# Layer 1: the low weights of two feature tiles side by side in the array's rows

## The chip, the cores and the metric

The kernel runs on one core of a Trainium2 chip. The metric is device time in microseconds of one execution, as the median of several. A profiled execution gives a trace of every instruction, and the line numbers (L508) are those of the kernel's source before the change. The engines are TensorE (PE for matmuls, PEld for weight loads), VectorE (DVE), ScalarE (ACT), GpSimd (POOL) and SyncE (SP, which here only issues transfers).

## The reference

An input of 2048 tokens by 576 features is normalised; a state-space convolution over the tokens (A) and a two-layer perceptron with another normalisation ahead of it (B) both work on the normalised input, and their results are multiplied.

```python
def _A_ref(u, log_A_real, A_imag, C_real, C_imag, log_dt, D_skip):
    ...
    P = jnp.exp((A * dt[:, None])[:, :, None] * pos[None, None, :])
    K = 2.0 * jnp.einsum("dn,dnl->dl", C, P).real
    ...
    y = jnp.fft.irfft(Uf * Kf[None, :, :], L2)[:, :, :L]
    ...
    return y + u * D_skip[None, None, :]

def _B_ref(x, w1, b1, w2, b2):
    y = _layernorm(x, axis=-1)
    h = _gelu(jnp.einsum("bsd,df->bsf", y, w1) + b1)
    return jnp.einsum("bsf,fd->bsd", h, w2) + b2

x = A_u
xn = _layernorm(x, axis=-1)
s = _A_ref(xn, ...)
g = _silu(_B_ref(xn, B_w1, B_b1, B_w2, B_b2))
return x + s * g
```

w1 is 576 x 4608 and w2 4608 x 576.

## The kernel before

**The perceptron.** To keep float32 accuracy in the fast matmul type, each operand is split into a high part (rounded) and a low part (the rest), and a product is taken as high x high, high x low and low x high. The tokens come in two halves of 1024, each half in two blocks of 512 (`tb` 0 and 1). The 4608 hidden features come in `NG` = 12 groups of `G` = 3 feature tiles of 128. One *slot* is one group with one token block, so there are 48 slots: for each half, for each group, `tb` 0 and then 1.

A slot has 11 positions. Positions 0 to 2 are layer 1 of feature tiles 0 to 2 (`layer1`, L508): 14 matmuls of 128 x 128 weights with 512 tokens each. The 576 input features are four full blocks of 128 and a rest of 64. The full blocks take 3 x 4 = 12 matmuls. For the rest the block `XR` holds the high part of the 64 rows in partitions 0 to 63 and their low part in 64 to 127, and there are two sets of weights: `w1r` has the high weights twice, so one matmul gives high x high and high x low; `w1s` has the low weights in partitions 0 to 63 and zeros below, so a second matmul gives low x high. Positions 3 to 10 are layer 2 (`layer2`, L565): 72 matmuls of 288 output columns for four token tiles j = 0 to 3, summed into `acc` by DVE (L573). The first group of a half adds the bias tile `bias2` instead of `acc`.

Layer 1 and layer 2 share two double banks of PSUM, `mxa` and `mxb`, by turns. Tile 0 and tile 2 of a slot use the two halves of one of them, tile 1 the other. Tile 1's is the one that token tile j = 3 of the slot before has used; it is free once the sum L573 of j = 3 is done.

**The convolution** is done in six chunks of 96 features with small matmuls in array tiles of 32 or 64 rows and columns, or 128 x 32: tables (`kgen`, L885, line `kl`), forward transforms (L958, line `c1`), second stage (L996, `c1`), inverse (L1049, `c3`) and last stage (L1076, `c3`). They are put as *visits* between the positions of a slot.

**The order** of all engines is fixed by a planner, `Order`, as the program is built. It keeps a clock for each engine (`od.t`), marks for finished steps (`od.marks`) and due times (`by`). TensorE's own sequence of positions is written out in the loop over slots at the end; `od.unit` puts down a block of matmuls with its planned length (`L1` for a feature tile, `LEN` for a position), `od.advance` puts down what other engines can do up to a time, and `pe_turns` makes the visits that are ready. All kinds of visits are allowed after positions 0, 1, 2, 4, 6, 8 and 10. `later(slot, pos, f)` runs f after a position.

Weights come from HBM through a ring `raw`, issued by SP (`load_raw`), and are split by ACT and DVE (`split_raw`, L485 and L488).

Of the kernel before, what the change touches and what calls it, by code (L numbers as in the profile page):

```python
# [9 lines left out]
F32 = mybir.dt.float32  # L10
F32R = mybir.dt.float32r
# [6 lines left out]
L, D, N, F = 2048, 576, 128, 4608  # L18
P = 128
# [19 lines left out]
TB = 512  # L39
# [173 lines left out]
def mixer_kernel(ctx, tc, u, log_a_real, a_imag, c_real, c_imag, log_dt, d_skip, w1, b1, w2, b2,  # L213
                 f1, f2, g2, g1, tvals, ident, out, parts=("mlp", "s4d")):
    nc = tc.nc
    sb = ctx.enter_context(tc.tile_pool(name="sb", bufs=1))
# [5 lines left out]
    def bank2(name):  # L222
        return ps.tile([P, 2, TB], F32, name=name, bufs=2 if name == "cv" else 1)

    def dram(ap_of, offset, ap):
        return bass.AP(tensor=ap_of.tensor, offset=ap_of.offset + offset, ap=ap)
# [22 lines left out]

    idt = ys_tile().rearrange("p i a b c -> p (i a b c)")[:, :P]  # L250
    idp = sb.tile([P, P], F32, name="idp")
    bias2 = sb.tile([P, D], F32, name="bias2")
    f1t = sb.tile([P, 2, 32], F32, name="f1t")
    g1t = sb.tile([P, 32], F32, name="g1t")
    tvs = sb.tile([P, NV + 7], F32, name="tv")
# [2 lines left out]
    halfpi, epst = small[:, 0:2], small[:, 2:4]  # L258
    dsk = sb.tile([P, D // 4], F32, name="dsk")
    w1s = sb.tile([P, G * P], F32R, name="w1s")  # L260

    def load_tv():
        for k in range(2):
# [51 lines left out]
    nc.vector.memset(halfpi, TWO_PI / 4)  # L315
    nc.vector.memset(epst[:, 0:1], EPS)
    nc.vector.memset(epst[:, 1:2], EPS * EPS)
    nc.vector.memset(w1s[64:].bitcast(F32), 0.0)
    nc.vector.memset(dsk, 0.0)


# [1 line left out]
    acc = sb.tile([P, 8, D], F32, name="acc")  # L323
# [77 lines left out]
    XR = sb.tile([P, 2, TB], F32R, name="XR")  # L401
# [27 lines left out]
    W = {}  # L429
# [33 lines left out]
    def split_raw(low_on=nc.vector):  # L463
        k = state["split"]
        state["split"] += 1
        half, g, which, i = PARTS[k]
        r = RAW.pop(k)
        if which == 1:
            if i == 0 and k:
                w1_tiles()  # L470
            h, lo, r1, r2 = W[1]
            if i < KB:
                h, lo = h[:, i], lo[:, i]
                m = P
            else:
                h, lo = r1, r2[:64]
                m = 64
        else:
            if i == 0:
                W[2] = (sb.tile([P, G, D], F32R, name="w2h"), sb.tile([P, G, D], F32R, name="w2l"))  # L480
            h, lo = W[2]
            h, lo, m = h[:, i], lo[:, i], P

        def low():
            low_on.tensor_sub(lo, r[:m], h[:m].bitcast(F32))  # L485
            for _ in range(NEXT[which - 1][i]):
                load_raw()
        nc.scalar.activation(h, r, AF.Copy)  # L488
        return low

    HID, LAST, Q1, Q2 = {}, {}, {}, {}
    turn = [0]

    def mx(i):
        return "mxa" if (turn[0] + i) % 2 == 0 else "mxb"

    def layer1(g, tb, i):
        h, lo, r1, r2 = W[1]
        c = slice(i * P, (i + 1) * P)
        if i < 2:  # L500
            Q1[i] = bank2(mx(i))
        q = Q1[i % 2][:, i // 2]
        ops = []
        for a, b in ((h, XH), (h, XL), (lo, XH)):
            ops += [(a[:, kb, c], b[:, kb, tb]) for kb in range(KB)]
        ops += [(r1[:, c], XR[:, tb]), (r2[:, c], XR[:, tb])]
        for j, (a, b) in enumerate(ops):
            nc.tensor.matmul(q, a, b, start=j == 0, stop=j == len(ops) - 1)  # L508
        return hidden(g, tb, i, q)

    def first_layer1(i):


        h, lo, r1, r2 = W[1]
        if i != 1:
            Q1[i] = bank2("mxb" if i else "mxa")
        q = Q1[2][:, 0] if i == 2 else Q1[0][:, i]
        pairs = [(h, XH, 0), (h, XH, 1), (h, XL, 0), (h, XH, 2), (h, XL, 1), (h, XH, 3), (h, XL, 2), (h, XL, 3)]

        if i != 1:  # L520
            for j, (a, b, kb) in enumerate(pairs):
                for k in ((0, 1), (2,))[i // 2]:
                    nc.tensor.matmul(Q1[k // 2 * 2][:, k % 2], a[:, kb, k * P:(k + 1) * P], b[:, kb, 0],  # L523
                                     start=j == 0, stop=False)
        c = slice(i * P, (i + 1) * P)
        for kb in range(KB):
            nc.tensor.matmul(q, lo[:, kb, c], XH[:, kb, 0], start=False, stop=False)
        for r in (r1, r2):
            nc.tensor.matmul(q, r[:, c], XR[:, 0], start=False, stop=r is r2)

        return [hidden(0, 0, k, Q1[k // 2 * 2][:, k % 2]) for k in ((), (0, 1), (2,))[i]]
# [18 lines left out]
    def layer2(g, tb, j, terms, last, alone=False):  # L550

        h, lo = W[2]
        hh, hl = HID[tb]
        c = slice(j * P, (j + 1) * P)
        if alone and terms[0][1]:
            Q2[j] = bank2("cv")
        elif j not in Q2:
            Q2[j] = bank2(mx(j + 1))  # L560
        q = Q2[j]
        for i, dh in terms:
            d = slice(dh * 288, dh * 288 + 288)
            for k, (a, b) in enumerate(((hh, h), (hh, lo), (hl, h))):
                nc.tensor.matmul(q[:, dh, :288], a[:, i, c], b[:, i, d], start=i == 0 and k == 0,  # L565
                                 stop=i == G - 1 and k == 2)
        if last:
            Q2.pop(j)

        def add(dh, n):  # L570
            o = acc[:, tb * 4 + j].rearrange("p (h d) -> p h d", h=2)[:, dh:dh + n]
            b = bias2.rearrange("p (h d) -> p h d", h=2)[:, dh:dh + n]
            nc.vector.tensor_add(o, q[:, dh:dh + n, :288], b if g == 0 else o)  # L573
        return add

    def tanh_half(z):
# [529 lines left out]
    NPOS = G + 8  # L1106
    NSLOT = 4 * NG
    od = Order(tc, nc)
    od.pinned = True
    el, wl2, wl, nl2, pl, pl2, pl3, pl4, pl5, nl, ml, ml2, xl, wx, c3, c2, c1, kl, tl, sl, vl, gl, fl, f2l = [od.line() for _ in range(24)]  # L1110
# [8 lines left out]
        load_raw()  # L1119
    for b in range(4, 8):  # L1120
        x_load(b)
    nc.sync.dma_start(bias2, dram(b2, 0, [[0, P], [1, D]]))

    zero = XL[:, KB - 1, 0]
    nc.gpsimd.memset(zero.bitcast(F32), 0.0)
# [58 lines left out]
    L1 = 14 * 0.2275  # L1184
    LEN = [L1] * G + [3 * n * 0.133 for n in (4, 2, 2, 4, 3, 3, 3, 3)]
# [86 lines left out]
    def x_free(tb):  # L1272
        od.marks["free", tb] = od.t["PE"] + od.LAT
        del od.marks["x", tb]
# [31 lines left out]
    def wmark(n, which):  # L1306

        per = KB + 1 + G
        a = n * per + (0 if which == 1 else KB + 1)
        return [("w", k) for k in range(a, a + (KB + 1 if which == 1 else G))]  # L1310
# [20 lines left out]
    part = {}  # L1331
    for k in range(4):
        gl["steps"].append(step("POOL", 5.0, lambda k=k: part.update({k: load_g2(k)}), mark=("g2", k),
                                need=[("g2c", k - 1)] if k else []))
# [37 lines left out]
    def pe_turns(limit=1, any_time=False, all_lines=True):  # L1372
        for x in (nl, pl, ml) + ((c3, c1, kl) if all_lines else ()):
            n = 0
            while n < (2 if x in (c1, nl) else limit):
                h = od.head(x)
                if h is None or h[0]["eng"] != "PE" or h[1] > od.t["PE"] + (0.3 if x is nl else -0.4):
                    break
                if x is c1:
                    now = od.t["PE"]  # L1380
                    gap = (END - now) / max(pace["left"], 1)
                    if n == 0 and pace["started"] and now < pace["last"] + 0.4 * gap and not any_time:
                        break
                    pace["started"], pace["last"] = True, now
                    pace["left"] -= 1
                if x is kl and pace["started"] and kl["steps"][0]["mark"][1] < NB - 1 and od.t["PE"] < h[1] + ALONE:
                    break
                behind = ride(h[0]) if x is c1 or x is c3 and h[0]["mark"][0] == "i1" else None
                od.run(x)
                if behind:  # L1390
                    behind()
                od.pin()
                od.advance(od.t["PE"])
                n += 1

    LATER = {}

    def later(slot, pos, f):
        LATER.setdefault((slot, pos), []).append(f)
    mid = 2 * NG  # L1400

    later(mid - 3, 0, block_lines)
    later(mid - 2, G - 1, lambda: x_free(0))
    later(mid - 1, G - 1, lambda: x_free(1))
    later(NSLOT - 10, 4, end_line)
# [41 lines left out]
    for slot in range(NSLOT):  # L1447
        turn[0] = slot + 1
        g, tb = slot // 2 % NG, slot % 2
        n = slot // 2  # L1450
        final = slot >= NSLOT - 2
        for pos in range(NPOS):
            if pos < G:
                need = wmark(n, 1) + [("x", tb)]
                if pos == 0:
# [4 lines left out]
                    if slot in (1, 2 * NG + 1):  # L1460
                        od.marks["x", tb] -= 2.3
                cell = []
                od.unit(lambda: cell.extend([layer1(g, tb, pos)] if slot else first_layer1(pos)),
                        L1 if slot else L1 * (22, 6, 14)[pos] / 14, need)
                look_ahead(pos)
                for k, (a, b, c) in enumerate(cell, pos + 1 - len(cell)):
                    by = hidden_by(pos, k)
# [6 lines left out]
            else:  # L1474
                j, terms, last, hid = l2_terms(pos - G)
                need = [wmark(n, 2)[i] for i in hid] + [("h", slot, i) for i in hid]
# [29 lines left out]
            for f in LATER.get((slot, pos), ()):  # L1506
                f()
            od.advance(od.t["PE"])
            pe_turns(all_lines=pos in (0, 1, 2, G + 1, G + 3, G + 5, NPOS - 1))
    od.force(lambda: not od.urgent and not any(x["steps"] for x in od.lines))  # L1510


# [52 lines left out]
```

## Time and profile before

| | |
|---|---|
| median of 3 runs | 1084.04 us (1083.93 to 1084.64) |
| profiled execution: its own time | 1084.01 us |
| profiled execution: its span, first to last instruction | 1082.2 us |
| mean granted TensorE clock | 0.998 |
| DVE busy | 945.4 us (87%) |
| ACT busy | 652.2 us (60%) |
| transfers | 125.55 MB, mean 116 GB/s |

The span is what the rows of the profile are measured in. Busy time counts each instruction from its start to its end, with overlapping ones joined; a matmul's end is modelled, so for TensorE the distance between starts tells more than the duration. In a group's row stand line, engine, operation, output and inputs, rows by columns of the array tile, shape, count, then busy time and mean duration in ns. In a timeline's row stand start and length in us; xN joins N like instructions. A wait's row has total, times and longest in us.

### The profile page before, as it was taken

Reading aid. Unit: us, or ns where it says so; the run is one execution under the profiler, and the core shown is the slowest. Engines: PE = TensorE matmul, PEld = TensorE weight load, DVE = VectorE, ACT = ScalarE, POOL = GpSimd, SP = SyncE. Lnnn points to the kernel's source line nnn. Section 1 sums busy time; section 2 is a strip of 40 time slices with the busy share of each in tenths; the row PEclk is TensorE's granted clock in tenths of the full one; section 3 lists DMA queues with packets and bytes.
Section 4 is the critical chain, followed back from the end, with each engine's and each line's share of the span. In section 5 each row is a group of like instructions: output and inputs, shape, how many; then the busy total and the mean of one; then the engine's idle time right before and its main releaser. Section 6 shows DMA issues by size and latency. Waiting matters only on the chain.

```text
span 1082.2 us, 27218 instructions
## 1 busy us (share of the span) xinstructions
PE 1073.0 (99%) x11507; PEld 935.6 (86%) x11507; DVE 945.4 (87%) x1520; ACT 652.2 (60%) x974; POOL 197.1 (18%) x282
## 2 busy tenths in 40 slices
PE   9999999999999999999999999999999999999997
PEld 7889989888888888898888888889888888888896
DVE  7799688988999998999999998998999897677266
ACT  6666678767576576557657767566665653233233
POOL 5592631111000100002100020000100013110420
PEclk9999999999999999999999999999999999999999
DMA  8654567424133321634525131241412347441623
GB/s 252 226 163 166 196 219 203 123 68 144 36 113 67 91 88 40 138 73 112 153 77 128 35 104 54 75 117 25 117 52 76 121 78 227 126 122 53 217 76 88
DMA packets 129371, 125.55 MB, mean 116 GB/s; under 512 B 78821, under 2 KB 100913, under 8 KB 128225
## 3 DMA queue, kind: packets, MB, share of 16 engines
q1 hardware_dynamic: 113584, 76.44, 25.4%
q0 software_dynamic: 15104, 46.49, 13.8%
q8 instruction: 90, 1.47, 0.5%
q10 hardware_dynamic: 560, 0.89, 0.3%
q14 instruction: 33, 0.26, 0.1%
HBM read 95.52 MB, written 34.01 MB: 120 GB/s over the span
## 4 chain that ended last, share of the span: by engine, by line
PE 97%; DVE 2%; ACT 0%; issue 0%; DMA 0%; ACTq 0%
PE mxa L508 21%; PE mxb L565 21%; PE mxb L508 21%; PE mxa L565 21%; PE cv L885 3%; PE cv L996 3%; PE cv L1049 2%; PE cv L958 2%; PE cv L1076 1%; PE mxa L523 0%; DVE st L371 0%; PE cv L413 0%; DVE row L386 0%; DMA acc<-in_A_u_dram 0%; DVE A L644 0%
## 5 line engine op out<-in xcount | busy, mean ns | idle before, releaser
L565 PE MATMUL mxb<-w2h,hh 128*128 128x288 f32 x576 | 171.7, 298 | 0.0
L565 PE MATMUL mxa<-w2h,hh 128*128 128x288 f32 x573 | 170.5, 297 | 0.0
L565 PE MATMUL mxb<-w2h,hl 128*128 128x288 f32 x576 | 170.2, 296 | 0.0
L565 PE MATMUL mxb<-w2l,hh 128*128 128x288 f32 x576 | 169.5, 294 | 0.0
L565 PE MATMUL mxa<-w2h,hl 128*128 128x288 f32 x573 | 169.1, 295 | 0.0
L565 PE MATMUL mxa<-w2l,hh 128*128 128x288 f32 x573 | 168.6, 294 | 0.0
L547 DVE TENSOR_TENSOR hl<-h,hh 128x512 fp32r<-128x512 f32 x144 | 98.8, 688 | 77.6 <-ACT hh L544 76.6
L541 ACT ACTIVATE h<-mxa,b1t 128x512 f32<-128x512 f32 x73 | 50.1, 688 | 125.5 <-PE mxa L508 123.6
L785 POOL DMA_DIRECT2D par<-par_s x36 | 27.4, 761 | 520.4 <-DVE mg L828 511.5
L565 PEld LDWEIGHTS mxa<-w2h,hh 128*128 128x128 f32 x573 | 107.6, 188 | 8.4 <-issue 4.1
L565 PEld LDWEIGHTS mxb<-w2h,hh 128*128 128x128 f32 x576 | 108.2, 188 | 6.8 <-issue 2.4
L565 PEld LDWEIGHTS mxb<-w2l,hh 128*128 128x128 f32 x576 | 108.2, 188 | 0.6
L565 PEld LDWEIGHTS mxb<-w2h,hl 128*128 128x128 f32 x576 | 108.1, 188 | 0.2
L565 PEld LDWEIGHTS mxa<-w2l,hh 128*128 128x128 f32 x573 | 107.6, 188 | 0.6
L565 PEld LDWEIGHTS mxa<-w2h,hl 128*128 128x128 f32 x573 | 107.5, 188 | 0.0
L541 ACT ACTIVATE h<-mxb,b1t 128x512 f32<-128x512 f32 x71 | 48.8, 687 | 79.9 <-PE mxb L508 79.0
L544 ACT ACTIVATE hh<-h 128x512 fp32r<-128x512 f32 x144 | 90.9, 632 | 4.2
L573 DVE TENSOR_TENSOR acc<-mxa,acc 128x576 f32<-128x576 f32 x88 | 65.4, 743 | 18.0 <-PE mxa L565 17.9
L508 PE MATMUL mxa<-XH,w1h 128*128 128x512 f32 x284 | 79.0, 400 | 0.0
L488 ACT ACTIVATE w2h<-raw 128x576 fp32r<-128x576 f32 x72 | 44.2, 674 | 56.6 <-PE mxa L565 56.4
L508 PE MATMUL mxb<-XH,w1h 128*128 128x512 f32 x280 | 77.8, 399 | 0.0
L508 PE MATMUL mxa<-XL,w1h 128*128 128x512 f32 x284 | 76.2, 390 | 0.0
(240 smaller groups left out, 2454.3 us busy)
## 6 DMA issues: line engine op xcount, KB each, us to landing
raw<-in_B_w_dram SPq DMA_DIRECT2D x72, 288.0 KB, 3.1
raw<-in_B_w_dram SPq DMA_DIRECT2D x96, 192.0 KB, 3.2
par_s<-A POOLq DMA_DIRECT2D x8, 1080.0 KB, 4.7
par<-par_s POOLq DMA_DIRECT2D x36, 240.0 KB, 3.3
f2t<-f2q SPq DMA_DIRECT2D x24, 256.0 KB, 3.4
raw<-in_B_w_dram SPq DMA_DIRECT2D x48, 96.0 KB, 3.9
xc<-xn_s SPq DMA_DIRECT2D x48, 96.0 KB, 3.7
u_s<-in_A_u_dram POOLq DMA_DIRECT2D x16, 288.0 KB, 4.4
```

Source lines behind the costliest of these rows:

```text
L488: nc.scalar.activation(h, r, AF.Copy)
L508: nc.tensor.matmul(q, a, b, start=j == 0, stop=j == len(ops) - 1)
L541: nc.scalar.activation(t, q, AF.Gelu_apprx_tanh, bias=b1t[:, g * G + i:g * G + i + 1], scale=1.0)
L544: LAST[0] = nc.scalar.activation(hh[:, i], t, AF.Copy)
L547: nc.vector.tensor_sub(hl[:, i], t, hh[:, i].bitcast(F32))
L565: nc.tensor.matmul(q[:, dh, :288], a[:, i, c], b[:, i, d], start=i == 0 and k == 0, stop=i == G - 1 and k == 2)
L573: nc.vector.tensor_add(o, q[:, dh:dh + n, :288], b if g == 0 else o)
L785: nc.gpsimd.dma_start(PAR[b].rearrange("p (g i) k -> p g (i k)", g=4), dram(par_s, (b // 6 * CH + b % 6 * 4) * NPAR, [[D * NPAR, P], [24 * ...
L885: nc.tensor.matmul(q[32 * g:32 * g + 32, i // 2, i % 2 * 64:i % 2 * 64 + 64], U[:, ri, 4 * g + i, :], v[:, ri, 4 * g + i, :], start=ri == ...
L958: nc.tensor.matmul(Q1ST[i, x][g // 2][64 * f:64 * f + 64, g % 2].rearrange(order), f1t[r].rearrange("p s k -> p (s k)"), rhs(r, f), start= ...
L996: nc.tensor.matmul(Q[i][32 * q:32 * q + 32, f, 2 * ri:2 * ri + 2], m[r, 4 * i + q, 32 * ri:32 * ri + 32], A2[r, 4 * p + 2 * i + q // 2, :, ...
L1049: nc.tensor.matmul(QI[q // 2][64 * f:64 * f + 64, q % 2, i], MAT["g2t", p + i // 2][r, i % 2, ri], YS[p + i // 2][0][r, i % 2, ri, f], sta ...
```

## The change

For some pairs of feature tiles the two low matmuls (`w1s` with `XR`) are taken out of their tiles and done together, as two matmuls of 64 rows that use the upper and the lower half of the array's rows: tile a from partitions 0 to 63, tile b from 64 to 127. So `w1s` holds the low weights in both halves of its partitions (the zeros go), and a second copy of the 64 high rows of `XR` lies in partitions 64 to 127 of a new tile, brought there by a transfer from SBUF to SBUF for each slot (`rows_again`). In a tile that is not paired, the matmul of `w1s` has all 128 rows as before, and adds the product low x low.

A pair is placed only where a visit of `kl`, `c1` or `c3` is the last thing that `pe_turns` has made: after position 0 (tiles 1 and 2 of the slot) or after position 10 (tiles 0 and 1 of the slot that follows; this asks for the sum of token tile 3). It comes first in its tiles' sums (`start=True`), and the tiles have 13 matmuls left. The copy is issued after position 1 of the slot before, for slots 3 to 22 and 27 to 47. Its tile takes the place of `bias2` in memory, so the bias is loaded once more in slot 23, ahead of the second half's first group.

```diff
-    bias2 = sb.tile([P, D], F32, name="bias2")
...
+    def bias_load():
+        PART["b2"] = sb.tile([P, D], F32, name="part")
+        nc.sync.dma_start(PART["b2"], dram(b2, 0, [[0, P], [1, D]]))
...
-    nc.vector.memset(w1s[64:].bitcast(F32), 0.0)
...
-                h, lo = r1, r2[:64]
-                m = 64
+                h, lo = r1, r2
+                m = P
...
+    def tile1(slot, i):
+        if (slot, i) not in OPEN:
+            if i < 2:
+                Q1[i] = bank2("mxa" if (slot + 1 + i) % 2 == 0 else "mxb")
+            OPEN[slot, i] = [Q1[i % 2][:, i // 2], False]
+        return OPEN[slot, i]
+
+    def side_by_side(slot, a, b):
+
+        tb = slot % 2
+        for i in sorted((a, b)):
+            tile1(slot, i)[1] = True
+        for i, r, x in ((a, slice(0, 64), XR[:64, tb]), (b, slice(64, P), PART["x2"][64:])):
+            nc.tensor.matmul(OPEN[slot, i][0], W[1][3][r, i * P:(i + 1) * P], x, start=True, stop=False)
+
+    def rows_again(slot):
+
+        if "x2" not in PART:
+            PART["x2"] = sb.tile([P, D], F32R, name="part")[:, 32:32 + TB]
+        nc.sync.dma_start(PART["x2"][64:].bitcast(F32), XR[:64, slot % 2].bitcast(F32))
+        od.marks["x2", slot] = od.t["PE"] + X2LOAD
+        od.pin()
...
-        ops += [(r1[:, c], XR[:, tb]), (r2[:, c], XR[:, tb])]
+        ops += [(r1[:, c], XR[:, tb])] + ([] if begun else [(r2[:, c], XR[:, tb])])
         for j, (a, b) in enumerate(ops):
-            nc.tensor.matmul(q, a, b, start=j == 0, stop=j == len(ops) - 1)
+            nc.tensor.matmul(q, a, b, start=j == 0 and not begun, stop=j == len(ops) - 1)
...
+                SEEN[0] = x is c3 or x is c1 or x is kl
                 n += 1
+
+    SEEN = [False]
+    X2LOAD, PAIR1 = 4.5, 0.33
+
+    def pair_up(slot, a, b, need):
+        now = od.t["PE"]
+        need = need + [("x2", slot), ("x", slot % 2)] + wmark(slot // 2, 1)
+        if not SEEN[0] or (slot, a) in OPEN or not all(od.marks.get(m, 1e9) <= now for m in need):
+            return
+        od.unit(lambda: side_by_side(slot, a, b), PAIR1, need)
+        for i in (a, b):
+            LEN[i] = L1 * 13 / 14
+        od.advance(od.t["PE"])
...
+    for s in [*range(2, mid - 2), *range(mid + 2, NSLOT - 1)]:
+        later(s, 1, lambda s=s: rows_again(s + 1))
+    later(mid - 1, 1, bias_again)
...
             od.advance(od.t["PE"])
+            SEEN[0] = False
             pe_turns(all_lines=pos in (0, 1, 2, G + 1, G + 3, G + 5, NPOS - 1))
+            if pos == 0:
+                pair_up(slot, 1, 2, [])
+            elif pos == NPOS - 1:
+                pair_up(slot + 1, 0, 1, [("acc", slot, 3, 0)])
```

More of the change, by code (lines that the diff above doesn't have):

```diff
@@ L260, in mixer_kernel @@
     w1s = sb.tile([P, G * P], F32R, name="w1s")
+    PART = {}
+    def bias_load():
+        PART["b2"] = sb.tile([P, D], F32, name="part")
+        nc.sync.dma_start(PART["b2"], dram(b2, 0, [[0, P], [1, D]]))
     def load_tv():
@@ L495, in mx, with layer1 @@
         return "mxa" if (turn[0] + i) % 2 == 0 else "mxb"
-    def layer1(g, tb, i):
+    OPEN = {}
+    def tile1(slot, i):
[16 more added lines that the diff above has]
+        od.pin()
+    def layer1(slot, g, tb, i):
         h, lo, r1, r2 = W[1]
         c = slice(i * P, (i + 1) * P)
-        if i < 2:
-            Q1[i] = bank2(mx(i))
-        q = Q1[i % 2][:, i // 2]
+        q, begun = tile1(slot, i)
         ops = []
@@ L571, in add @@
             o = acc[:, tb * 4 + j].rearrange("p (h d) -> p h d", h=2)[:, dh:dh + n]
-            b = bias2.rearrange("p (h d) -> p h d", h=2)[:, dh:dh + n]
-            nc.vector.tensor_add(o, q[:, dh:dh + n, :288], b if g == 0 else o)
+            b = PART["b2"].rearrange("p (h d) -> p h d", h=2)[:, dh:dh + n] if g == 0 else o
+            nc.vector.tensor_add(o, q[:, dh:dh + n, :288], b)
         return add
@@ L1121, in mixer_kernel @@
         x_load(b)
-    nc.sync.dma_start(bias2, dram(b2, 0, [[0, P], [1, D]]))
+    bias_load()
     zero = XL[:, KB - 1, 0]
@@ L1400, in mixer_kernel, with bias_again @@
     mid = 2 * NG
+    def bias_again():
+        PART.pop("x2")
+        bias_load()
+        od.pin()
     later(mid - 3, 0, block_lines)
+    for s in [*range(2, mid - 2), *range(mid + 2, NSLOT - 1)]:
+        later(s, 1, lambda s=s: rows_again(s + 1))
+    later(mid - 1, 1, bias_again)
     later(mid - 2, G - 1, lambda: x_free(0))
@@ L1462, in mixer_kernel @@
                 cell = []
-                od.unit(lambda: cell.extend([layer1(g, tb, pos)] if slot else first_layer1(pos)),
-                        L1 if slot else L1 * (22, 6, 14)[pos] / 14, need)
+                od.unit(lambda: cell.extend([layer1(slot, g, tb, pos)] if slot else first_layer1(pos)),
+                        LEN[pos] if slot else L1 * (22, 6, 14)[pos] / 14, need)
+                LEN[pos] = L1
                 look_ahead(pos)
```

## The prediction

> **What bounds the kernel now.** I read the page's busy table and its chain of waits first, because they say which engine a saved instruction has to be on.
>
> ```profile
> PE 1073.0 (99%) x11507; PEld 935.6 (86%) x11507; DVE 945.4 (87%) x1520; ACT 652.2 (60%) x974; POOL 197.1 (18%) x282
> ...
> PE 97%; DVE 2%; ACT 0%; issue 0%; DMA 0%; ACTq 0%
> ```
>
> TensorE is busy 99% of the 1082.2 us span and carries 97% of the chain that ends last. So a matmul taken away shortens the run by what it occupies, and one put in lengthens it. The longest entry in the view of PE's waits agrees, 1.3 us before the warm-up at the start:
>
> ```profile
> PE mxa L1131 <- POOL XL L1125: 1.3, 1, 1.3
> ```
>
> DVE at 87% is not the bound, but it can become one for single waits.
>
> Next, the groups by form, for the instructions that the change is about, the products of `w1s`:
>
> ```profile
> L508 PE MATMUL mxa<-XR,w1s 128*128 128x512 f32 x71 | 27.6, 389 | 0.0
> ...
> L508 PE MATMUL mxb<-XR,w1s 128*128 128x512 f32 x70 | 27.2, 388 | 0.0
> ```
>
> 141 of them, one for each feature tile of slots 1 to 47. The 389 ns is latency: matmuls overlap. What one occupies is the distance from start to start, and that comes from the timeline of TensorE, here one tile before a convolution visit (L958), the visit, and the tile after it:
>
> ```profile
> 220.26 0.39 PE L508 MATMUL mxa<-XR,w1r 128*128 128x512 f32 x1
> 220.49 0.39 PE L508 MATMUL mxa<-XR,w1s 128*128 128x512 f32 x1
> 220.81 0.90 PE L958 MATMUL cv<-xc,f1t 32*64 32x384 f32 x16
> 221.64 1.20 PE L508 MATMUL mxb<-XH,w1h 128*128 128x512 f32 x4
> 222.67 1.07 PE L508 MATMUL mxb<-XL,w1h 128*128 128x512 f32 x4
> 223.58 1.07 PE L508 MATMUL mxb<-XH,w1l 128*128 128x512 f32 x4
> 224.49 0.39 PE L508 MATMUL mxb<-XR,w1r 128*128 128x512 f32 x1
> 224.72 0.39 PE L508 MATMUL mxb<-XR,w1s 128*128 128x512 f32 x1
> 224.94 0.29 PE L565 MATMUL mxa<-w2h,hh 128*128 128x288 f32 x1
> ```
>
> Three things stand in these rows. In the stream four matmuls take 223.58 - 222.67 = 0.91 us, so one takes 0.2275. From the last full matmul to the visit's first there are 220.81 - 220.49 = 0.32 us, 0.09 more than 0.2275: going over to another shape of tile costs 0.09. And after the visit the first four need 222.67 - 221.64 = 1.03, 0.12 more than 0.91: the first weights of a new shape can't be loaded under a running matmul.
>
> **What a pair saves and costs.** It saves two matmuls of the stream, 2 x 0.2275 = 0.455 us (the two tiles then have 13 each). It adds two matmuls of 64 rows by 128 columns. The trace has few of that shape, L693, and they show what the change of rows alone costs:
>
> ```profile
> 37.48 0.40 PE L508 MATMUL mxa<-XR,w1s 128*128 128x512 f32 x1
> 37.72 0.60 PE L692 MATMUL cv<-ys,kt 128*128 128x128 f32 x4
> 38.25 0.27 PE L693 MATMUL cv<-ys,kt 64*128 64x64 f32 x1
> 38.45 0.73 PE L508 MATMUL mxb<-XH,w1h 128*128 128x512 f32 x2
> ```
>
> From L508 to L692 the shape stays and the distance is the ordinary one (0.24). The four L692 last 0.60 with 0.27 for the last, so they start (0.60 - 0.27) / 3 = 0.11 apart and the last at 38.05; L693, with the same 128 columns and half the rows, comes 0.20 later, 0.09 too late. From L693 back to L508 it is 0.20 again for half as long a stream (0.055): a switch and weights loaded in the open. And the second L508 then starts at 38.45 + 0.73 - 0.39 = 38.79, 0.34 after the first, 0.11 more than 0.2275. So 128 to 64 rows is a switch, in both directions.
>
> A visit is followed by one switch now (visit to full array, 0.09, first weights 0.11). With a pair it is followed by two: visit to 64 rows, then 64 rows to the full array. The first takes the place of the present one. The pair's own bill is therefore: its first weights in the open 0.11, one stream of 512 elements for both 0.21 to 0.2275, the second's later start 0.01, and one more switch 0.09; the full tile's first weights lay open before as well. Sum 0.42 to 0.44, I take 0.43. Gain per pair 0.455 - 0.43 = 0.025 us: nearly all of the saving goes into the second switch and the open weights. The planner's own price, PAIR1 = 0.33, holds the open weights and one stream, and no second switch.
>
> That the halves run at once I take from the visit above: 16 matmuls of 384 elements pass in 221.64 - 220.81 = 0.83 us with the switch; one after another, at L692's 0.11 for 128, they would need 16 x 0.33 = 5.3. These are of another number type and half as fast per element, so a pair at full rate is not shown.
>
> **How many pairs.** They are made only where a convolution visit (kl, c1 or c3) is the last thing after tile 0 or at the end of a slot, in slots that have the copy: 3 to 22 and 27 to 47. I counted along the timeline, 42 products of L508 and 72 of L565 to a slot. After tile 0 there are 14 such visits, the first and the last being
>
> ```profile
> 195.04 1.10 PE L885 MATMUL cv<-v,U 128*32 128x64 f32 x64
> ...
> 1000.36 1.61 PE L1076 MATMUL cv<-A,g1t 64*32 64x384 f32 x32
> ```
>
> At slot ends there are 9, three of them ahead of slots already counted (a slot gets one pair), 20 slots in all. The first and the last of the 9 begin with
>
> ```profile
> 395.95 1.10 PE L885 MATMUL cv<-v,U 128*32 128x64 f32 x64
> ...
> 974.40 1.60 PE L996 MATMUL cv<-A,f2t 64*32 64x192 f32 x64
> ```
>
> At a slot's end the pair also asks that the sum of the last token tile (L573) be done, since it frees tile 1's bank. Two visits, of TensorE and then of DVE:
>
> ```profile
> 906.90 0.90 PE L958 MATMUL cv<-xc,f1t 32*64 32x384 f32 x16
> 907.73 0.50 PE L508 MATMUL mxb<-XH,w1h 128*128 128x512 f32 x1
> ...
> 488.37 1.10 PE L885 MATMUL cv<-v,U 128*32 128x64 f32 x64
> 489.40 0.50 PE L508 MATMUL mxb<-XH,w1h 128*128 128x512 f32 x1
> ```
>
> ```profile
> 907.01 0.76 DVE L573 TENSOR_TENSOR acc<-mxa,acc 128x576 f32<-128x576 f32 x1 [2.46 <-PE mxa L565]
> ...
> 489.10 0.74 DVE L573 TENSOR_TENSOR acc<-mxa,acc 128x576 f32<-128x576 f32 x1
> ```
>
> In the first the sum ends at 907.77, 0.04 after the visit; in the second at 489.84, 0.44 after it, and the planner would refuse that pair. The longer visits cover the sum. So I take 19 pairs: 19 x 0.025 = 0.5 us gained. The new wait at slot ends, with the whole of the tile's matmuls queued behind it on TensorE, I put at 0.1 us in two or three places where the planner's clock is a little off: 0.2 us back. Its bounds are 0 and 0.44 at six of the nine slot ends, the planner refusing the rest, 2.6 us.
>
> **What is hidden.** 41 copies of 64 rows by 2 KB (128 KB each) go through SP's queue. The nearest issue, and the longest entry of that queue's own waits:
>
> ```profile
> g2t<-g2p SPq DMA_DIRECT2D x24, 128.0 KB, 3.1
> ...
> SPq L448 <- DVE w1l L485: 395.4, 25, 33.0
> ```
>
> A landing takes about 3 us, and the copy is issued after tile 1 of the slot before: tile 2, 14 x 0.2275 = 3.2 us, and all of layer 2 lie between it and the pair. It waits for the pair that last read the tile, which stands earlier in TensorE's order; behind it on SP are the weight loads of `raw`, and these sit waiting for DVE (395 us in all, the second row), so they lose nothing. If that cover were gone, a copy that is late by its landing would cost 3 us at one pair. The bias comes back by one more load, in slot 23 for slot 24, a slot ahead. The fill of `w1s` that goes away and the low half, now 128 rows instead of 64 with as many elements in each, cost DVE and POOL what they did or less:
>
> ```profile
> L485 DVE TENSOR_TENSOR w1s<-raw,w1r x23: 541/544/549, 49.9 to 1032.2; 64x384 fp32r<-64x384 f32 x23
> ...
> L318 DVE MEMSET w1s<- x1: 378/378/378, 1.1 to 1.1; 64x384 f32 x1
> ```
>
> 0.378 us at 1.1 us, when TensorE only warms up: nothing. A pair at a slot's end needs the new weights' low part 3 us earlier than now. The planner asks for it too, and it is split a whole layer 2 before. What is left is the order of other work, which the planner writes anew from its altered clock. Each stop of TensorE costs 0.09 + 0.09 + 0.11 = 0.29 us, so three stops more or less are 0.9 us, either way.
>
> The sum goes against the profiled execution's own time, 1084.01 us (span 1082.2); the median of the runs shown, 1084.04, is the same to 0.03. 1084.0 - 0.5 + 0.2 = 1083.7 us.
>
> **The rivals.** First, the second switch or the open weights are hidden. A pair is then 0.32 to 0.34, gains 0.12, 19 x 0.12 = 2.3 us: 1081.7. For it speaks that weights of other tiles in the same shape are loaded together in the visits; against it the L692, L693, L508 rows, where each change of rows shows its 0.09.
>
> Second, a pair costs no more than one matmul, 0.2275 + 0.01, and gains 0.22: 19 x 0.22 = 4.2, 1079.8 us. The Trainium skill, "TensorE: Matmul & The Clock Gate", Part 3, has this rule: tiles in different row groups take the span of one matmul and about 4 ns for each further one. By that rule the second rival's time would come out; the rows of L693 speak against it at this place, as the pair stands between two changes of shape.
>
> Third, slower: the halves run one after the other, because full-rate streams of 512 into two banks are not taken side by side. A pair is then 0.43 + 0.2275 = 0.66, loses 0.2, 19 x 0.2 = 3.9: 1087.9 us. A pair makes the kernel slower from 0.455 up, and by over 0.2% from 0.455 + 2.17 / 19 = 0.57. Against it speak the 0.83 us of the sixteen; for it, that no row has such a pair.
>
> Fourth, the pairs are rarely made, as the planner's clock leaves out most places: 1084.0, no change. It lies inside the forecast.
>
> **How the numbers follow.** 0.2% is 2.17 us, about what a measurement of this kernel can tell from no change. Forecast with the fourth rival 0.60, of which 0.52 lie within 2.17 us and 0.08 above it, from slot-end waits near their bound with a worse order of stops. First rival 0.20, of which 0.17 faster by over 0.2% and 0.03 within, its 2.3 us being so near to 2.17. Second 0.05, faster; third 0.15, slower. Faster 0.17 + 0.05 = 0.22, same 0.52 + 0.03 = 0.55, slower 0.08 + 0.15 = 0.23. The range 1081.2 to 1087.0 takes in the first rival, and above it the waits' bound of 2.6 us with three more stops (1084.0 - 0.5 + 2.6 + 0.9). It leaves out the second rival and the third at its full price: 2 in 10.
>
> **What would show it.** In the timeline after: 64-row matmuls of `w1s` with `part` behind visits, some 19 times two. The distance from the pair's first start to the next full matmul's start should be 0.42 to 0.44, with both halves starting 0.01 apart. 0.33 means the first rival, 0.24 the second, 0.65 the third. Matmuls of the full `w1s` should fall from 141 by twice the number of pairs. I am wrong if the pair's distance is outside 0.38 to 0.50, if PE's waits show DVE L573 or the copy for more than 1 us in all, or if the number of stops moves by more than five.

## The result and the profile after

The changed kernel takes 1087.21 us (median of 9 runs) against 1084.04 us before: the ratio is 1.003, 95% interval 1.0021 to 1.0039. It is slower, and lies 0.2 us above the range; the forecast was 1083.7. (Ratios leave disturbed runs out, so they can differ a little from the quotient of two medians.) The profiled execution took 1087.15 us, its span is 1085.4 us, 3.2 longer than before.

The page's busy table and the engines of its chain:

```profile
PE 1073.5 (99%) x11507; PEld 931.1 (86%) x11507; DVE 945.0 (87%) x1519; ACT 654.1 (60%) x976; POOL 197.1 (18%) x282
...
PE 94%; DVE 2%; ACT 2%; issue 1%; DMA 0%; ACTq 0%; DVEq 0%
```

TensorE still sets the time, but its share of the chain has gone from 97% to 94%, and ScalarE now has 2% where it had none. The groups by form show how many pairs there are (L535 is the old L508, L516 the pair):

```profile
L535 PE MATMUL mxa<-XR,w1s 128*128 128x512 f32 x48 | 18.7, 389 | 0.0
...
L535 PE MATMUL mxb<-XR,w1s 128*128 128x512 f32 x47 | 18.3, 388 | 0.0
...
L516 PE MATMUL mxa<-XR,w1s 64*128 64x512 f32 x12 | 6.0, 498 | 0.0
L516 PE MATMUL mxb<-part,w1s 64*128 64x512 f32 x12 | 5.9, 493 | 2.2 <-ACT h L568 2.2
L516 PE MATMUL mxb<-XR,w1s 64*128 64x512 f32 x11 | 5.5, 499 | 0.0
L516 PE MATMUL mxa<-part,w1s 64*128 64x512 f32 x11 | 5.4, 495 | 0.0
```

23 pairs, and 141 - 46 = 95 whole low matmuls. One of the pair's groups has idle time before it, 2.2 us, and what ended it is the GELU (ACT, L568). The waits of TensorE say the same:

```profile
PE mxb L516 <- ACT h L568: 2.2, 3, 1.0
PE cv L417 <- DVE U L385: 1.4, 1, 1.4
PE mxa L1158 <- POOL XL L1152: 1.3, 1, 1.3
```

The first row did not exist before. The second is of the start-up, before the first matmuls of layer 1, where the kernel before waited 0.6 us for DVE. Two pairs in the timeline of TensorE, one of the ordinary kind and one of those three, and ScalarE beside the second:

```profile
195.23 1.10 PE L912 MATMUL cv<-v,U 128*32 128x64 f32 x64
196.26 0.50 PE L516 MATMUL mxb<-XR,w1s 64*128 64x512 f32 x1
196.26 0.50 PE L516 MATMUL mxa<-part,w1s 64*128 64x512 f32 x1
196.69 0.73 PE L535 MATMUL mxb<-XH,w1h 128*128 128x512 f32 x2
...
217.78 0.90 PE L985 MATMUL cv<-xc,f1t 32*64 32x384 f32 x16
218.61 0.50 PE L516 MATMUL mxa<-XR,w1s 64*128 64x512 f32 x1
220.12 0.49 PE L516 MATMUL mxb<-part,w1s 64*128 64x512 f32 x1 [1.01 <-ACT h L568]
220.54 0.73 PE L535 MATMUL mxa<-XH,w1h 128*128 128x512 f32 x2
```

```profile
216.93 1.14 ACT L847 ACTIVATE w<-w,tv 128x1024 f32<-128x1024 f32 x1
218.08 1.28 ACT L568 ACT_TABLE_LOAD   x1
219.38 0.69 ACT L568 ACTIVATE h<-mxb,b1t 128x512 f32<-128x512 f32 x1
```

The ordinary pair: both halves start together, and the next full matmul 196.69 - 196.26 = 0.43 us later. The other one: the second half starts at 220.12, 1.51 us after the first, and 0.05 after the end of the GELU at 219.38 + 0.69 = 220.07. That GELU reads the sum of tile 0, which lies in one bank of `mxb`; the waiting matmul writes tile 2's sum into the other bank of the same double bank. The GELU is late since ScalarE had a 1024-element piece of the tables and a table load of 1.28 us ahead of it.

The view of waits counts only 1.01 us there, because the first half's modelled end covers 0.5 of it. From start to start the three late pairs lose 1.50, 0.87 and 1.28 us, 3.65 in all:

```profile
309.64 0.50 PE L516 MATMUL mxa<-XR,w1s 64*128 64x512 f32 x1
310.50 0.49 PE L516 MATMUL mxb<-part,w1s 64*128 64x512 f32 x1 [0.37 <-ACT h L568]
...
496.79 0.50 PE L516 MATMUL mxa<-XR,w1s 64*128 64x512 f32 x1
498.07 0.49 PE L516 MATMUL mxb<-part,w1s 64*128 64x512 f32 x1 [0.78 <-ACT h L568]
```

Two more pairs after tile 0 were held for a moment, by 0.09 and 0.02 us from start to start, too little for the view of waits. The longer of them, TensorE and then ScalarE:

```profile
891.74 0.50 PE L516 MATMUL mxb<-XR,w1s 64*128 64x512 f32 x1
891.83 0.49 PE L516 MATMUL mxa<-part,w1s 64*128 64x512 f32 x1
```

```profile
891.09 0.69 ACT L568 ACTIVATE h<-mxa,b1t 128x512 f32<-128x512 f32 x1
```

Here too the second half starts 0.05 us after the GELU's end, 891.83 against 891.78, as it does at all five places. The five pairs at slot ends wait for nothing: their halves start 0.003 us apart, and the waits for DVE's sum that were expected there are not seen.

The sum is then 1084.04 - 23 x 0.025 + 3.65 + 0.11 (the two short waits) = 1087.2 us. That it meets the measured time to 0.1 us is partly luck: in the profiled executions the first tile of slot 1 starts at 34.64 us, 0.20 later than before, and the sum does not have that.

### The profile page after: what moved, and what is told of

Its sections match the earlier page's. It is cut to its first block, busy times and chain, and to the rows that moved or that the text cites. A ratio compares the mean times of both kernels' runs of the same rounds, so it can differ in the third digit from the quotient of the medians.

```text
span 1085.4 us, 27304 instructions
## 1 busy us (share of the span) xinstructions
PE 1073.5 (99%) x11507; PEld 931.1 (86%) x11507; DVE 945.0 (87%) x1519; ACT 654.1 (60%) x976; POOL 197.1 (18%) x282
## 4 chain that ended last, share of the span: by engine, by line
PE 94%; DVE 2%; ACT 2%; issue 1%; DMA 0%; ACTq 0%; DVEq 0%
PE mxa L535 21%; PE mxa L592 20%; PE mxb L592 20%; PE mxb L535 20%; PE cv L1023 3%; PE cv L912 3%; PE cv L1076 2%; PE cv L985 2%; PE cv L1103 1%; PE mxb L516 1%; ACT w2h L492 0%; PE cv L417 0%; PE mxa L550 0%; PE mxa L516 0%; ACT L568 0%
## 5 line engine op out<-in xcount | busy, mean ns | idle before, releaser
L592 PE MATMUL mxb<-w2h,hh 128*128 128x288 f32 x576 | 171.7, 298 | 0.0
L592 PE MATMUL mxa<-w2h,hh 128*128 128x288 f32 x573 | 170.6, 298 | 0.0
L592 PE MATMUL mxb<-w2h,hl 128*128 128x288 f32 x576 | 170.2, 296 | 0.0
L592 PE MATMUL mxb<-w2l,hh 128*128 128x288 f32 x576 | 169.5, 294 | 0.0
L592 PE MATMUL mxa<-w2h,hl 128*128 128x288 f32 x573 | 169.1, 295 | 0.0
L592 PE MATMUL mxa<-w2l,hh 128*128 128x288 f32 x573 | 168.6, 294 | 0.0
L568 ACT ACTIVATE h<-mxa,b1t 128x512 f32<-128x512 f32 x73 | 50.1, 687 | 139.0 <-PE mxa L535 137.1
L592 PEld LDWEIGHTS mxb<-w2h,hh 128*128 128x128 f32 x576 | 108.1, 188 | 7.8 <-issue 3.1
L592 PEld LDWEIGHTS mxa<-w2h,hh 128*128 128x128 f32 x573 | 107.6, 188 | 7.7 <-issue 2.5
L592 PEld LDWEIGHTS mxb<-w2l,hh 128*128 128x128 f32 x576 | 108.1, 188 | 0.6
L592 PEld LDWEIGHTS mxb<-w2h,hl 128*128 128x128 f32 x576 | 108.1, 188 | 0.2
L592 PEld LDWEIGHTS mxa<-w2l,hh 128*128 128x128 f32 x573 | 107.6, 188 | 0.6
L592 PEld LDWEIGHTS mxa<-w2h,hl 128*128 128x128 f32 x573 | 107.5, 188 | 0.0
L568 ACT ACTIVATE h<-mxb,b1t 128x512 f32<-128x512 f32 x71 | 48.8, 688 | 85.7 <-PE mxb L535 84.9
L535 PE MATMUL mxa<-XH,w1h 128*128 128x512 f32 x284 | 78.9, 399 | 0.0
L535 PE MATMUL mxb<-XH,w1h 128*128 128x512 f32 x280 | 78.0, 400 | 0.0
L535 PE MATMUL mxa<-XL,w1h 128*128 128x512 f32 x284 | 76.1, 390 | 0.0
L535 PE MATMUL mxa<-XH,w1l 128*128 128x512 f32 x284 | 75.9, 389 | 0.0
```

What stands on the lines that cost most here:

```text
L535: nc.tensor.matmul(q, a, b, start=j == 0 and not begun, stop=j == len(ops) - 1)
L568: nc.scalar.activation(t, q, AF.Gelu_apprx_tanh, bias=b1t[:, g * G + i:g * G + i + 1], scale=1.0)
```

## The experiments

Theory G: the 3 us are the waits of the pair's second matmul for the GELU of tile 0; the pair itself gains its 0.025 us. Rival O: the planner's new order, or the copies on SP's queue, cost them. Rival P: pairs cost more than they save. The first four kernels ran on one chip, where the kernel before took 1084.67 us.

**Pairs only where the planner has the GELU done.** The planner gets a mark for it, and the pair after tile 0 asks for the mark.

```diff
-                    od.urgent.append((od.t["PE"], [step("ACT", 0.62, a, tbl="gelu", by=by[0]),
+                    od.urgent.append((od.t["PE"], [step("ACT", 0.62, a, tbl="gelu", mark=("g", slot, k), by=by[0]),
...
-                pair_up(slot, 1, 2, [])
+                pair_up(slot, 1, 2, [("g", slot, 0)])
```

> The pair after tile 0 is placed only where the planner's clock has the GELU of tile 0 done; 19 pairs are made instead of 23. Theory G (the pair's second matmul waits on TensorE until ScalarE has read tile 0's sum out of the same double bank; three late GELUs cost 3.65 us in the changed kernel): those waits go, each pair is worth 0.02 to 0.03 us, so 1083.4 to 1084.1 us. Rival O (the planner's new order of visits, or the copies on SP's queue, cost the 3 us, and the waits only show slack elsewhere): 1086 to 1087.3 us, as the copies and an altered order stay. Rival P (a pair costs more than it saves): over 1086 us.

Measured 1084.09 us, ratio to the kernel before 0.9997 (0.9989 to 1.0006), with 19 pairs. All the waits of TensorE:

```profile
PE mxa L1158 <- POOL XL L1152: 1.3, 1, 1.3
PE cv L417 <- DVE U L385: 0.9, 1, 0.9
PE mxa L550 <- ACT XH L421: 0.2, 1, 0.2
```

No pair shows in it (one second half starts 0.015 us after the first, the others 0.003 or 0.004), and the loss is gone with 19 pairs and all the copies in place. P falls. So does O as the cause in the changed kernel: TensorE makes its visits here at the same places of the order as there, and the GELU of slot 10's tile 0 ends as late, at 220.11 us for 220.07; with no pair at that place, nothing loses time. The medians differ by 0.58 us (19 x 0.025 = 0.48 was expected), which the interval doesn't tell from nothing.

**Pairs only at slot ends, and only after tile 0.** One of the two calls of `pair_up` is left out in each.

```diff
-            if pos == 0:
-                pair_up(slot, 1, 2, [])
-            elif pos == NPOS - 1:
+            if pos == NPOS - 1:
                 pair_up(slot + 1, 0, 1, [("acc", slot, 3, 0)])
```

> Pairs only at the ends of slots, none after tile 0; 6 pairs, and all copies. Theory G: no wait for GELU is left, as tile 0's GELU has not begun when the pair runs; 6 x 0.025 = 0.15 us gained: 1083.7 to 1084.3 us. Rival O: above 1086 us if the copies are the cause; if it is the order, anything from 1083 to 1087. Rival P: 6/23 of the 3.2 us, 1084.9 us.

Measured 1084.89 us, ratio 0.9999 (0.9990 to 1.0008), 6 pairs, none waiting for a GELU; one waits 0.09 us for DVE's sum. The median is 0.6 us above the upper figure of G, as the kernel before is on this chip, and it is the very figure of P; P has fallen with the kernel above, and the ratio shows no loss.

> Pairs only after tile 0, none at slot ends; 19 pairs. Theory G: the late GELUs at the places of the changed kernel stay, 3.0 to 3.9 us of waits less 19 x 0.025: 1086.5 to 1087.6 us, and the trace shows the second matmul of three or four pairs starting 0.05 us after a GELU's end. Rival O: no fixed relation, waits and time differ. Rival P: 19/23 of 3.2, 1086.7 us with the loss spread evenly over the pairs.

Measured 1089.33 us, ratio 1.0038 (1.0026 to 1.0050), 19 pairs. That is above what G gave. Its waits of TensorE, the rows that are not at the start:

```profile
PE mxb L516 <- ACT h L568: 1.4, 2, 1.0
...
PE mxa L592 <- DVE acc L600: 0.7, 1, 0.7
PE mxb L592 <- DVE acc L600: 0.6, 1, 0.6
PE mxa L592 <- DVE hl L574: 0.4, 1, 0.4
```

The GELU waits are there at the same two first places (1.51 and 0.87 us from start to start), the third has gone because the order differs. But layer 2 (L592) now waits 1.7 us for DVE, which the views of the other kernels do not have, and TensorE makes its visits in another order than in the change. So rival O is right for a part of this kernel: each new order can bring waits of its own.

**Everything but the pairs.** Both calls of `pair_up` are left out.

> The whole change but no pair is placed: copies by SP, the shared tile for bias and copy, the low weights in both halves of the rows, with all low matmuls whole. Theory G and rival P: the rest costs nothing, 1083.8 to 1084.4 us. Rival O with the copies as the cause: 1086 us or more.

Measured 1085.16 us, ratio 1.0005 (0.9996 to 1.0014). The copies, the shared tile and the wider low weights cost nothing that shows, within 1.5 us. TensorE's visits are in the order of the kernel before, so this kernel says nothing of the new order. The median is 0.8 us above the upper figure expected; on this chip the kernel before is 0.6 higher too.

**Is it the bank or the bookkeeping?** Each double bank becomes two tiles of one bank each. DVE then needs two instructions of 288 for a sum that took one of 576. The next three kernels ran on one chip; the kernel before took 1084.78 us there.

```diff
+    class Two:
+        def __init__(self, name):
+            self.half = [ps.tile([P, TB], F32, name=f"{name}{k}", bufs=1) for k in range(2)]
...
     def bank2(name):
+        if name != "cv":
+            return Two(name)
...
-            nc.vector.tensor_add(o, q[:, dh:dh + n, :288], b)
+            for e in range(dh, dh + n):
+                o = acc[:, tb * 4 + j, e * 288:e * 288 + 288]
+                b = PART["b2"][:, e * 288:e * 288 + 288] if g == 0 else o
+                nc.vector.tensor_add(o, q[:, e, :288], b)
```

> The change with all its pairs (23), but each double bank of mxa and mxb is two tiles of one bank for the dependence tracking; the sum of layer 2 (L573 before) is therefore two DVE instructions of 288 instead of one of 576, some 0.1 us more DVE work in each of 192 sums. Theory G1 (the wait is an artefact of tracking two banks as one tile): the second matmul of every pair starts within 0.02 us of the first unless DVE's sum holds it, with GELUs as late as before, and TensorE waits 0 us for GELU. Against the kernel with two tiles and no pairs it is 23 x 0.025 = 0.6 us faster, within -0.1 to 1.2. Rival G2 (the neighbour bank can't be written while ScalarE reads, whatever is tracked): the late pairs still stand 0.9 to 1.5 us, 2 to 4 us slower than without pairs.

Measured 1087.04 us, with all 23 pairs. The pair that answers to the one at 218.61 above, TensorE and ScalarE (here L526 is the pair and L578 the GELU):

```profile
220.66 0.90 PE L996 MATMUL cv<-xc,f1t 32*64 32x384 f32 x16
221.49 0.50 PE L526 MATMUL mxa<-XR,w1s 64*128 64x512 f32 x1
221.49 0.50 PE L526 MATMUL mxb<-part,w1s 64*128 64x512 f32 x1
221.92 0.96 PE L545 MATMUL mxa<-XH,w1h 128*128 128x512 f32 x3
```

```profile
219.92 1.14 ACT L858 ACTIVATE w<-w,tv 128x1024 f32<-128x1024 f32 x1
221.07 1.28 ACT L578 ACT_TABLE_LOAD   x1
222.37 0.69 ACT L578 ACTIVATE h<-mxb,b1t 128x512 f32<-128x512 f32 x1
```

The GELU is as late as in the change, begins 0.88 us after the pair, and the pair does not wait: 0.43 us, as all 23 here (0.425 to 0.434). At this place the matmul is done before the GELU begins, so the one bank of `mxb` is not read while the other is written. The pair that answers to the one at 891.74 shows that case:

```profile
891.56 0.50 PE L526 MATMUL mxb<-XR,w1s 64*128 64x512 f32 x1
891.56 0.49 PE L526 MATMUL mxa<-part,w1s 64*128 64x512 f32 x1
```

```profile
891.11 0.69 ACT L578 ACTIVATE h<-mxa,b1t 128x512 f32<-128x512 f32 x1
```

The GELU reads tile 0's bank of `mxa` until 891.80, and the second half, into the other bank, starts 0.004 us after the first, 0.24 before the GELU's end. In the change it waited for that end. So it was the bookkeeping (G1), not the bank (G2).

> The reference for the kernel with two tiles: two tiles of one bank each, the sum in two DVE instructions, and no pairs. Both theories: near the time of the kernel before, 1083.5 to 1088 us, as the split sum adds up to 20 us of DVE work (87% busy now) and may cause waits of its own.

Measured 1087.86 us, 0.82 more than with the pairs (0.6 was expected). The sign is as reckoned, but the single runs of each kernel spread over more than 2 us, so the two medians do not show the size of the gain. Against the kernel before both are slower, 1.0020 (1.0012 to 1.0029) and 1.0024 (1.0015 to 1.0033); without pairs, slot 1 begins 3.05 us later than before and the distance then stays between 3.0 and 3.7 us, so the two-tile form loses its time at the start. Which of its instructions does that there was not tried.

**The change once more**, beside these two.

> The change as it is, once more, beside the others on one chip. Both theories: 3 us slower than before, with the same three pairs of 0.9 to 1.5 us that end 0.05 us after a GELU.

Measured 1087.43 us, ratio 1.0025 (1.0016 to 1.0034). The late pairs are the same three, with 1.51, 0.88 and 1.25 us.

## Why the prediction was wrong

The step that failed is the one on waits in "How many pairs": it asked what the pairs at slot ends would wait for, and charged those after tile 0 with no wait at all. The pair's second matmul there writes tile 2's sum into the double bank that tile 0's GELU still reads. Tile 2 had that wait before as well, but tile 1's 14 matmuls lay in front of it and covered it. The pair takes that cover away. Both halves of this could be found in the kernel and the trace of before. Tile 0 and tile 2 are two halves of one PSUM tile, and tile 2's first weight load, after the visit at 220.81, carries a wait on ScalarE:

```profile
221.64 0.53 PEld L508 LDWEIGHTS mxb<-XH,w1h 128*128 128x128 f32 x3 [0.60 <-ACT h L541]
```

The row names the GELU, L541. It does not show that the GELU held the load: ScalarE's rows are

```profile
219.67 0.69 ACT L541 ACTIVATE h<-mxb,b1t 128x512 f32<-128x512 f32 x1
...
220.92 0.68 ACT L541 ACTIVATE h<-mxa,b1t 128x512 f32<-128x512 f32 x1
```

Tile 0's GELU (`mxb`) had ended at 220.36; tile 1's (`mxa`) only ended last, and the matmul comes 0.83 us after the visit's first, as it does behind the like visit at 906.90. At one of the 14 places counted, though, ScalarE was late already, TensorE first, ScalarE second:

```profile
492.80 1.59 PE L1076 MATMUL cv<-A,g1t 64*32 64x384 f32 x32
494.31 0.97 PE L508 MATMUL mxa<-XH,w1h 128*128 128x512 f32 x3
```

```profile
493.56 1.28 ACT L541 ACT_TABLE_LOAD   x1
494.85 0.69 ACT L541 ACTIVATE h<-mxb,b1t 128x512 f32<-128x512 f32 x1
```

The visit ends at 494.31 and the GELU at 495.54, 1.23 us later; in the change this pair lost 1.28. The other two late places came because visits moved: those at 217.78 and 307.88 stood after tile 1 in the kernel before (220.81 and 309.48), where no pair is placed.

Point by point. The price of a pair, 0.42 to 0.44, was right: 0.428 to 0.434 for the 18 that nothing held, both halves 0.003 or 0.004 us apart. So the second switch is paid, as the rows of L693 said, and the first two rivals fall with it. The Trainium skill ("TensorE: Matmul & The Clock Gate", Part 3) gives packed tiles the span of one matmul and about 4 ns for each further one. The trace agrees on the 4 ns; the pair as a whole takes 0.43 us of the stream and not the 0.2275 of one matmul. The third rival falls by the same rows: the halves run at once. The gain of 0.025 us per pair follows from that price; the medians have its sign and are too scattered to show its size. The number of pairs was 23 for 19, as the moved visits gave 18 places after tile 0 for 14; that moves 0.1 us. The wait at slot ends was put at 0.2 us and is nothing in the change; the kernel with pairs at slot ends alone has one of 0.09. The copies were right to be costed at nothing: with all of them and no pairs the ratio is 1.0005, and they land in 3.7 us:

```profile
part<-XR SPq DMA_DIRECT2D x41, 128.0 KB, 3.7
```

The planner's order was allowed 0.9 us for stops; the number of stops went from 78 to 79. It can cost more than that, as the kernel with pairs after tile 0 alone shows, but not here: the first kernel of the experiments has the change's order of visits and no loss. The sign came out on the side that had 0.23, and by a mechanism that was not among the rivals; that the third rival's 1087.9 lies near the measured time is chance.

## What to carry to other kernels

When work is moved forward on the engine that sets the time, list every wait that its instructions already have, not only the ones that look new: a wait that never showed may have been covered by exactly the work that now comes later. Then look for the latest case of the releasing engine in the trace, not the usual one; three of 23 pairs made nearly the whole loss. A tile that spans two banks was one thing to the dependence tracking here, so put into it only what may wait for one another.

## What the runs showed of the hardware that was not expected

Two streams of 512 into two banks, from the two halves of the array's rows, run side by side: 0.425 to 0.434 us a pair with its open weights and the switch, where 0.66 was reckoned for one after the other, and a start 0.003 or 0.004 us apart where 0.01 was reckoned. And ScalarE's reading of one bank did not hold TensorE's start on the other, once each bank was a tile of its own (891.11 to 891.80 and 891.56 in the two-tile kernel).
